# A quarter of V weighted on VectorE and folded on GpSimd, in a decode block with cached keys and values

## The chip, the core and the metric

The kernel runs on one core of a Trainium2 chip. The metric is the device time of one execution in microseconds (us), the median of several runs. A core has five engines that run side by side, each with its own queue of instructions taken in order: TensorE (PE, matrix products), VectorE (DVE), ScalarE (ACT), GpSimd (POOL) and SyncE (SP, which here only issues transfers). Sixteen DMA engines move data between the large memory (HBM) and the core's own memory of 128 partitions. Engines wait for each other by semaphores.

## The reference

Two requests (B = 2), one new token each, width 512, 32 heads of 128, and a cache of 8192 keys and values per head in fp32. The block computes, cut to what matters:

```python
y = layernorm(x)
q = (y @ wq)                       # 32 heads of 128
scores = einsum("bhqd,bhkd->bhqk", q, k_cache) * Dh ** -0.5
p = softmax(scores)
o = einsum("bhqk,bhkd->bhqd", p, v_cache)
h = x + o @ wo                     # wo: 4096 x 512
out = h + gelu(layernorm(layernorm(h)) @ w1 + b1) @ w2 + b2
```

K and V are 268 MB each and are read once. Each value of them is used in one multiplication.

## The kernel before, in words

Two heads and one request make one iteration: 16 pairs of heads times 2 requests are 32 iterations, `i` = 0 to 31. For each, `load` brings a K tile and a V tile of 128 partitions by 128 rows by 128 elements (8.39 MB). Partition `p` of the first 64 belongs to the first head and holds 128 consecutive rows of its cache; the other 64 belong to the second head. Three buffers (`kv`, tag `kv`) go round over wq, K0, V0, K1, V1 and so on, so a tile is loaded when the tile three places before it has been used up: V of iteration i+1 waits for the sums of K of iteration i, and K of iteration i+1 waits for the use of V of iteration i-1. All these loads stand in SyncE's queue in that order, and behind them the weights of the second half (`ws`).

Scores of iteration i are computed in four chunks of 32 rows. `multiply` (line 246) multiplies a chunk of K by q in place on VectorE. `halve` (256) adds the upper 64 elements of each row to the lower 64 on GpSimd, for the rows that `split` gives it (32, 32, 32 and 12), and `sums` (266) reduces what is left on VectorE, one chunk behind. In the last three iterations ScalarE sums some rows too (`by_act`, 260), and GpSimd halves 22, 22, 22 and 8. `row_max` and `all_max` (270 to 280) find the maximum over partitions through TensorE, and `exps` (291) writes the exponentials of the iteration just done into `ptz`, zero-padded to eight columns so that one product serves both heads.

`values(done)` (314) multiplies V of the iteration before by those exponentials: 32 products of 128x8 by 128x512 into four row groups of a PSUM tile `so`. `gather` copies `so` out on ScalarE, `head_sum` (335) adds up the four groups and four column blocks, `head_out` (350) divides by the sum of the exponentials and sets rows in the order in which `turn` and `turned` (358, 367) multiply them by rows of wo. wo comes in nine groups after `PLAN`. Five of them are gathered by an indirect transfer from GpSimd's queue (`load_wo`, 144 and 145) that leaves 32 partitions out, eight blocks of four.

`make_q` (231) spreads q over the partitions with products against `pick`: one call serves two pairs of heads and takes four products, one for each head of a pair and each request. At the end, iteration 31 has its V loaded in four pieces; the softmax, the last products, the two layer norms and the two products with w1 and w2 follow on a chain in which `keep_warm` and `stay_awake` put in products that nobody reads. The order on each engine is that of the program, with `behind` (issue_after) placing one instruction after another. In the loop, `all_max(done)`, `exps(done)` and `values(done)` come ahead of the first `multiply(i, 0)`, and `multiply(i, 0)` is placed behind `all_max`'s reduction.

Of the kernel before, what the change touches and what calls it, by code (L numbers as in the profile page):

```python
# [26 lines left out]
NG = 4  # L27
WARM = 4
MOST = 20
WR = 4  # L30


PLAN = [4, (4, 16, 68, 72, 76, 80, 84, 88),
# [4 lines left out]
FAR = 4096  # L38


# [1 line left out]
def tile_decode_block(ctx: ExitStack, tc: tile.TileContext, x, k, v, wq, wo, w1, b1, w2, b2, out):  # L42
    nc = tc.nc
    B, H, SK, DH = k.shape
    D = x.shape[-1]
    F = w1.shape[1]
    HP = P // QG
    NS = SK // HP
    NC = NS // CH
    DC = D // P  # L50
# [26 lines left out]

    wqt = kv.tile([P, DC, H * DH], F32, name="wqs", tag="kv")
    nc.sync.dma_start(wqt, wq.rearrange("(p r) n -> p r n", r=DC))

    ident = const.tile([P, P], F32, name="ident")
    make_identity(nc, ident)
# [11 lines left out]
    groups, at = [], 0  # L94
    for blocks in PLAN:
        shut = blocks if isinstance(blocks, tuple) else None
        r = WR if shut else blocks
        n = (P - 4 * len(shut or ())) * r
        groups.append((at, n, r, shut))
        at += n  # L100
    assert at == HL * DH
    kept = [[p for p in range(P) if not any(s0 <= p < s0 + 4 for s0 in shut or ())] for _, _, _, shut in groups]
# [4 lines left out]
    part = const.tile([P, 1], F32, name="part")  # L107
# [4 lines left out]
    for _, _, _, blocks in groups:  # L112
        if blocks and blocks not in index:
            acc = work.tile([P, 1], F32, name="ixf")
            nc.vector.tensor_copy(acc, part)
            ends = [p for s0 in blocks for p in (s0, s0 + 4)]
            for p in sorted(set(ends)):
                if ends.count(p) == 1:
                    if p in blocks:
                        edge, step, first = p, FAR, p  # L120
                    else:
                        edge, step = p, first - p - FAR
                    one = work.tile([P, 1], F32, name="ix1")
                    nc.vector.tensor_scalar(one, part, edge - 0.5, float(step), op0=ALU.is_ge, op1=ALU.mult)
                    nc.vector.tensor_add(acc, acc, one)
# [22 lines left out]

    epst = const.tile([P, 1], F32, name="epst")
    nc.vector.memset(epst, EPS)  # L150
    eps2 = const.tile([P, 1], F32, name="eps2")
    nc.vector.memset(eps2, EPS * EPS)
# [6 lines left out]
    QR = 32 * (QG - 1) + B  # L159
# [7 lines left out]
    sel_all = sel.rearrange("p e j -> p (e j)")  # L167
# [5 lines left out]
    nc.vector.memset(sel_row, 0.0)  # L173
    for e in range(QG):
        nc.vector.tensor_copy(sel_row[:, :, 32 * e + B - 1], sel[:, e, :])
    pt2 = const.tile([P, 2, NS // 4, 4 * QG], F32, name="pt")
    nc.gpsimd.memset(pt2, 0.0)
    ptz = [pt2[:, j] for j in range(2)]

    WB = 32 // B  # L180
    otl = const.tile([P, QG, 32], F32, name="otl")
    nc.vector.memset(otl, 0.0)
    place = const.tile([B, 32], F32, name="place")
    nc.vector.memset(place, 0.0)
    nc.vector.tensor_copy(place[:, ::WB], ident[:B, :B])
    sv = const.tile([P, 32], F32, name="sv")
    nc.vector.memset(sv, 0.0)
# [20 lines left out]
    pick = const.tile([P, B, HP], F32, name="pick")  # L208
    nc.vector.tensor_copy(pick, sel_all[:, :B, None].to_broadcast([P, B, HP]))

    QW = H * DH // NG
    q2 = const.tile([P, QW], F32, name="q2")
    for r in range(DC):
        for j in range(QW // 512):
            for n in range(NG):
                nc.tensor.matmul(so2[j][32 * n:32 * n + B], yT[:, r, :],
                                 wqt[:, r, n * QW + j * 512:n * QW + (j + 1) * 512],
                                 start=(r == 0), stop=(r == DC - 1))
    for j in range(QW // 512):
        nc.scalar.activation(q2[:, j * 512:(j + 1) * 512], so2[j], AF.Copy)  # L220

    qps = {}

    def make_q(m):
        n, at = divmod(QG * m * DH, QW)
        t = psq.tile([P, 512], F32, name="qps").rearrange("p (t b d) -> p t b d", t=2, b=B)
        qps[m], qps[m + 1] = t[:, 0], t[:, 1]
        rows = q2[32 * n:32 * n + B, at:at + 2 * QG * DH].rearrange("b (t e d) -> b t e d", t=2, e=QG)
# [9 lines left out]
    ST, MX, MT, GM, GI, LT, RL, SS, OP, TP = {}, {}, {}, {}, {}, {}, {}, {}, {}, {}  # L238
    wl = q2.rearrange("p (e n) -> p e n", e=QG)

    def multiply(i, c):
# [41 lines left out]
    def exps(i):  # L283
        m, b = divmod(i, B)
        nb = work.tile([P, QG], F32, name="nb")
        nc.scalar.activation(nb, GM.pop(i), AF.Copy, scale=SCALE)  # L286
        LT[m] = lt2[:, m % 2]
        s = ST.pop(i).rearrange("p (u j) -> p u j", j=4)
        for e in range(QG):
            ps = slice(e * HP, (e + 1) * HP)  # L290
            nc.scalar.activation(ptz[i % 2][ps, :, 4 * e:4 * e + 4], s[ps], AF.Exp, bias=nb[ps, e:e + 1], scale=SCALE,  # L291
                                 accum_out=LT[m][ps, 32 * e + b:32 * e + b + 1])
# [14 lines left out]
            RL[i] = rl  # L307
            return last

    def values(i, us=range(NS // 4)):  # L310
        so = so2[i % 2]
        for u in us:
            n = u % NG
            m = nc.tensor.matmul(so[32 * n:32 * n + 4 * QG], ptz[i % 2][:, u, :], vt[i][:, 4 * u:4 * u + 4, :],  # L314
                                 start=(u < NG), stop=(u >= NS // 4 - NG))
        return m

    def gather(i):
        SS[i] = work.tile([P, 512], F32, name="ss", bufs=3)
# [50 lines left out]
    def behind(m):  # L370
        return tc.issue_after(m.ins)
# [12 lines left out]
    kt, vt = {}, {}  # L384
# [3 lines left out]
    for i in range(NI):  # L388
        m, b = divmod(i, B)
        done = i - 1  # L390
# [26 lines left out]
        for c in range(NC):  # L417
# [24 lines left out]
            if late and c == 1:  # L442
                spare = psq.tile([P, 512], F32, name="spare", tag="qps")
# [11 lines left out]
        if late:  # L455
            with behind(awake):
                last = values(done, range(MOST))
# [4 lines left out]

    hl = NI - 1
    wt = kv.tile([P, 2, NS * DH // 2], F32, name="ws", tag="kv")
    w1t = wt[:, 0, :DC * F].rearrange("p (c f) -> p c f", c=DC)
    w1v = w1.rearrange("(p c) f -> p c f", c=DC)
    for c in range(0, DC, 2):
# [18 lines left out]
    with behind(after):  # L486
        ended = inverse(hl)
    gather(hl - 1)
    junk = const.tile([P, 2], F32, name="junk")
# [18 lines left out]
    nc.vector.tensor_scalar(basec, base, bmean, None, op0=ALU.subtract)  # L508

    wb = ident.bitcast(BF16)  # L510
    wp = spare[:, :2 * P]

    def keep_warm(n):
        for _ in range(n):
            m = nc.tensor.matmul(wp, wb[:, :P], wb, start=True, stop=True)
        return m


# [51 lines left out]
    hs = pick.rearrange("p b q -> p (b q)")  # L570
# [16 lines left out]
    for c in range(DC):  # L587
# [5 lines left out]
        last = m  # L593
# [57 lines left out]
```

## Time and profile before

| | us |
|---|---|
| median of 3 runs | 1307.65 (1307.62 to 1308.06) |
| span of the profiled execution | 1305.9 |
| its VectorE, GpSimd, TensorE busy | 932.7, 494.2, 446.8 |
| moved by DMA | 561.50 MB, mean 430 GB/s |

The profiled execution has no time of its own beside its span, from the first to the last instruction; the median of the runs is 1.7 us above that span. The page gives the busy time of each engine, the span in 40 slices, the transfer queues, the chain of work that ended last, and the costliest groups of instructions with mean duration and with what ended the idle time before them. "kv<-kv,qps" names the output and the inputs of an instruction; L246 is line 246. Where "x2" follows a row of a timeline, two instructions have been merged into it.

### The profile page before, as it was taken

Reading aid. Unit: us, or ns where it says so; the run is one execution under the profiler, and the core shown is the slowest. Engines: PE = TensorE matmul, PEld = TensorE weight load, DVE = VectorE, ACT = ScalarE, POOL = GpSimd, SP = SyncE. Lnnn points to the kernel's source line nnn. Section 1 sums busy time; section 2 is a strip of 40 time slices with the busy share of each in tenths; the row PEclk is TensorE's granted clock in tenths of the full one; section 3 lists DMA queues with packets and bytes.
Section 4 is the critical chain, followed back from the end, with each engine's and each line's share of the span. In section 5 each row is a group of like instructions: output and inputs, shape, how many; then the busy total and the mean of one; then the engine's idle time right before and its main releaser. Section 6 shows DMA issues by size and latency. Waiting matters only on the chain.

```text
span 1305.9 us, 7466 instructions
## 1 busy us (share of the span) xinstructions
PE 446.8 (34%) x2934; PEld 130.9 (10%) x2934; DVE 932.7 (71%) x551; ACT 98.6 (8%) x431; POOL 494.2 (38%) x151
## 2 busy tenths in 40 slices
PE   3033313333332334413342232333323334123468
PEld 0001001010010101001010010101001011000113
DVE  3666688757688666787766787666787667797891
ACT  0000000000000000000000000000000000004440
POOL 0433344532344432444332454333444433453330
PEclk9566556766566666656766566666666666566689
DMA  9999999999999999999999999999999999999998
GB/s 418 426 440 428 438 422 444 424 440 426 442 426 440 428 438 428 426 444 430 436 426 438 430 434 436 424 442 424 440 426 432 438 432 436 429 428 429 428 434 351
DMA packets 12727, 561.50 MB, mean 430 GB/s; under 512 B 1568, under 2 KB 1584, under 8 KB 2484
## 3 DMA queue, kind: packets, MB, share of 16 engines
q1 hardware_dynamic: 11968, 557.08, 98.8%
q0 software_dynamic: 720, 3.93, 0.7%
q8 instruction: 23, 0.38, 0.1%
q14 instruction: 12, 0.10, 0.0%
q10 hardware_dynamic: 4, 0.00, 0.0%
HBM read 562.32 MB, written 0.00 MB: 431 GB/s over the span
## 4 chain that ended last, share of the span: by engine, by line
DMA 43%; DVE 24%; issue 14%; PE 12%; POOL 5%; ACT 1%; SPq 0%; POOLq 0%; DVEq 0%
DMA kv<-in_A_k_cache_dram 38%; DVE kv L246 14%; PE so L314 10%; DVE s L266 9%; POOL kv L256 5%; DMA kv<-in_A_v_cache_dram 3%; DMA ws<-in_B_w_dram 1%; ACT pt L291 1%; PE rowacc L367 1%; DVE orow L350 1%; PE sm L280 1%; PE sm L273 0%; DVE gm L277 0%; DVE mx L270 0%; ACT nb L286 0%
## 5 line engine op out<-in xcount | busy, mean ns | idle before, releaser
L246 DVE TENSOR_TENSOR kv<-kv,qps 128x4096 f32<-128x4096 f32 x128 | 562.4, 4415 | 313.8 <-DMA kv<-in_A_k_cache_dram 313.6
L256 POOL TENSOR_TENSOR kv<-kv 128x2048 f32<-128x2048 f32 (+3 forms) x128 | 476.8, 3734 | 754.1 <-DVE kv L246 566.3
L266 DVE TENSOR_REDUCE s<-kv 128x32 f32<-128x2048 f32 (+5 forms) x160 | 325.3, 2066 | 10.9 <-POOL kv L256 10.6
L314 PE MATMUL so<-kv,pt 128*8 128x512 f32 x2048 | 280.8, 709 | 42.7 <-ACT pt L291 37.3
L273 PE MATMUL sm<-ident,mx 128*1 128x128 f32 x32 | 10.9, 340 | 446.0 <-DVE mx L270 446.0
L314 PEld LDWEIGHTS so<-kv,pt 128*8 128x8 f32 x2048 | 56.4, 101 | 239.5 <-issue 194.3
L367 PE MATMUL rowacc<-wog,ot 128*2 128x512 f32 x70 | 50.3, 881 | 64.8 <-DVE ot L365 33.4
L286 ACT ACTIVATE nb<-sm 128x2 f32<-128x2 f32 x32 | 5.5, 172 | 851.4 <-PE sm L280 851.4
L231 PE MATMUL qps<-q,pick 2*64 2x256 f32 x64 | 13.8, 577 | 127.6 <-DVE kv L246 127.6
L273 PEld LDWEIGHTS sm<-ident,mx 128*1 128x1 f32 x32 | 2.5, 79 | 472.5 <-issue 278.0
L358 PE MATMUL sm<-ident,orow 2*128 2x2 f32 x35 | 5.2, 244 | 130.1 <-DVE orow L350 130.1
L320 ACT ACTIVATE ss<-so 128x512 f32<-128x512 f32 x31 | 18.5, 598 | 269.6 <-PE so L314 269.6
L260 ACT ACTIVATE kv<-kv 128x128 f32<-128x128 f32 x114 | 33.5, 295 | 24.2 <-DVE kv L246 21.4
L335 PE MATMUL sm<-ss,selr 128*34 128x128 f32 x240 | 28.7, 273 | 0.0
L291 ACT ACTIVATE pt<-s,nb 64x128 f32<-64x128 f32 x64 | 25.5, 399 | 1.4
L335 PEld LDWEIGHTS sm<-ss,selr 128*34 128x34 f32 x240 | 25.1, 112 | 0.0
L260 ACT ACTIVATION_READ_ACCUMULATOR kv<-kv 128x1 f32 x114 | 21.3, 186 | 0.0
L280 PE MATMUL sm<-gm,ones 1*128 1x2 f32 x64 | 16.6, 326 | 11.9 <-DVE gm L277 11.9
L277 DVE TENSOR_REDUCE gm<-sm 1x2 f32<-1x128 f32 x32 | 8.9, 279 | 16.2 <-PE sm L273 16.2
L231 PEld LDWEIGHTS qps<-q,pick 2*64 2x64 f32 x64 | 5.5, 192 | 136.9 <-DVE kv L246 133.2
L358 PEld LDWEIGHTS sm<-ident,orow 2*128 2x128 f32 x35 | 4.4, 207 | 132.6 <-DVE orow L350 79.9
L367 PEld LDWEIGHTS rowacc<-wog,ot 128*2 128x2 f32 x70 | 6.8, 107 | 97.9 <-issue 64.1
(110 smaller groups left out, 169.2 us busy)
## 6 DMA issues: line engine op xcount, KB each, us to landing
kv<-in_A_k_cache_dram SPq DMA_DIRECT2D x4, 4096.0 KB, 32.9
ws<-in_B_w_dram SPq DMA_DIRECT2D x3, 1792.0 KB, 18.5
kv<-in_A_v_cache_dram SPq DMA_DIRECT2D x1, 4096.0 KB, 33.4
wog<-in_A_wo_dram SPq DMA_DIRECT2D x3, 1024.0 KB
kv<-in_A_v_cache_dram SPq DMA_DIRECT2D x1, 2048.0 KB, 37.9
kv<-in_A_v_cache_dram SPq DMA_DIRECT2D x1, 1536.0 KB, 41.2
ws<-in_B_w_dram SPq DMA_DIRECT2D x1, 1024.0 KB, 17.0
wog<-in_A_wo_dram SPq DMA_DIRECT2D x1, 512.0 KB
```

The costliest lines, as they stand in the source:

```text
L231: nc.tensor.matmul(t[e * HP:(e + 1) * HP, :, b], pick[32 * n:32 * n + B, b, :], rows[:, :, e], start=True, stop=True)
L246: return nc.vector.tensor_tensor(kc, kc, qb, op=ALU.mult)
L256: nc.gpsimd.tensor_tensor(t[:, :, :DH // 2], t[:, :, :DH // 2], t[:, :, DH // 2:], op=ALU.add)
L260: nc.scalar.activation(kt[i][:, j, :], kt[i][:, j, :], AF.Copy, accum_out=ST[i][:, j:j + 1])
L266: nc.vector.tensor_reduce(ST[i][:, a:e], kt[i][:, a:e, :d], axis=AX.X, op=ALU.add)
L273: nc.tensor.transpose(MT[i], mx, ident)
L280: GI[i] = nc.tensor.matmul(GM[i], ones[:1, :], gm, start=True, stop=True)
L291: nc.scalar.activation(ptz[i % 2][ps, :, 4 * e:4 * e + 4], s[ps], AF.Exp, bias=nb[ps, e:e + 1], scale=SCALE, accum_out=LT[m][ps, 32 * e + ...
L314: m = nc.tensor.matmul(so[32 * n:32 * n + 4 * QG], ptz[i % 2][:, u, :], vt[i][:, 4 * u:4 * u + 4, :], start=(u < NG), stop=(u >= NS // 4 - ...
L320: return nc.scalar.activation(SS[i], so2[i % 2], AF.Copy)
L335: nc.tensor.matmul(OP[m], sel_row[:, j, B - 1 - c:B - 1 - c + QR], SS[i - 1 + c][:, j * DH:(j + 1) * DH], start=(c == 0 and j == 0), stop= ...
L367: nc.tensor.matmul(rowacc, t[:, r, :], wo_g[g][:, r, :], start=False, stop=(g == len(groups) - 1 and r == n - 1))
```

## The change

1. In iterations 1 to 30, the last 32 of the 128 rows per partition of V are no longer multiplied on TensorE. `weigh` adds the two columns of `ptz` that hold a row's exponential (one of them is zero), multiplies the 32 rows of V by them on VectorE, and GpSimd adds the 32 rows in three steps (16, 8 and 4 rows) down to four. `values_folded` multiplies rows 0 to 95 by 24 products as before, and the four folded rows by one product against `whose`, which is one for the partitions of each head. `multiply(i, 0)` is now placed behind the weighting. The last two values products (iterations 30 and 31) are as before.
2. `make_q`: q of both heads of a pair stand in one row group pair, and one product per request serves both heads (16 products in all where there were 32); wq is read in another order for it.
3. `keep_warm`: products of 512 columns where there were products of 256, half as many.
4. `PLAN`: the 32 partitions left out of each gathered group are given as runs of any length instead of blocks of four.
5. x is loaded on ScalarE's queue after a first square root (which loads ScalarE's table), not as the first instruction of all.
6. `otl`, `sv` and `place` lie in the unused end of the tile `ws` and are set by GpSimd near the end.

The core of the diff:

```diff
-PLAN = [4, (4, 16, 68, 72, 76, 80, 84, 88),
+PLAN = [4, ((10, 18), (51, 3), (73, 3), (84, 8)),
...
-    x2 = work.tile([B, D], F32, name="x2", tag="ss", bufs=3)
-    nc.scalar.dma_start(x2, x.rearrange("b s d -> (b s) d"))
...
+    first = nc.scalar.activation(junk[:, 0:1], eps2, AF.Sqrt)
+    x2 = work.tile([B, D], F32, name="x2", tag="ss", bufs=3)
+    with tc.issue_after(first.ins):
+        nc.scalar.dma_start(x2, x.rearrange("b s d -> (b s) d"))
...
         for b in range(B):
-            for e in range(QG):
-                nc.tensor.matmul(t[e * HP:(e + 1) * HP, :, b], pick[32 * n:32 * n + B, b, :], rows[:, :, e],
-                                 start=True, stop=True)
+            nc.tensor.matmul(t[:, :, b], pick[part, b, :],
+                             q2[part, at:at + 2 * DH].rearrange("r (t d) -> r t d", t=2), start=True, stop=True)
...
+    def weigh(i):
+        w = s_of[i][:, FOLD:].rearrange("p (u j) -> p u j", j=4)
+        pt = ptz[i % 2][:, FOLD // 4:]
+        nc.vector.tensor_tensor(w, pt[:, :, 0:4], pt[:, :, 4:8], op=ALU.add)
+        t = vt[i][:, FOLD:]
+        last = nc.vector.tensor_tensor(t, t, s_of.pop(i)[:, FOLD:, None].to_broadcast([P, NS - FOLD, DH]),
+                                       op=ALU.mult)
+        n = (NS - FOLD) // 2
+        while n >= 4:
+            nc.gpsimd.tensor_tensor(t[:, :n], t[:, :n], t[:, n:2 * n], op=ALU.add)
+            n //= 2
+        return last
+
+    def values_folded(i):
+        so = so2[i % 2]
+        values(i, range(FOLD // 4), range(FOLD // 4 - NG + 1, FOLD // 4))
+        n = FOLD // 4 % NG
+        nc.tensor.matmul(so[32 * n:32 * n + 4 * QG], whose.rearrange("p e j -> p (e j)"), vt[i][:, FOLD:FOLD + 4, :],
+                         start=False, stop=True)
...
             last = all_max(done)
             exps(done)
             if not late:
-                values(done)
+                with behind(last):
+                    last = weigh(done)
+                values_folded(done)
...
-        for _ in range(n):
-            m = nc.tensor.matmul(wp, wb[:, :P], wb, start=True, stop=True)
+        for j in range(0, n, 2):
+            t = min(2, n - j)
+            m = nc.tensor.matmul(wp[:, :t * 2 * P], wb[:, :P], wb[:, None, :].to_broadcast([P, t, 2 * P]),
+                                 start=True, stop=True)
```

More of the change, by code (lines that the diff above doesn't have):

```diff
@@ L79, in tile_decode_block @@
     nc.sync.dma_start(wqt, wq.rearrange("(p r) n -> p r n", r=DC))
+    eps2 = const.tile([P, 1], F32, name="eps2")
+    nc.vector.memset(eps2, EPS * EPS)
+    junk = const.tile([P, 2], F32, name="junk")
+    first = nc.scalar.activation(junk[:, 0:1], eps2, AF.Sqrt)
+    x2 = work.tile([B, D], F32, name="x2", tag="ss", bufs=3)
+    with tc.issue_after(first.ins):
+        nc.scalar.dma_start(x2, x.rearrange("b s d -> (b s) d"))
     ident = const.tile([P, P], F32, name="ident")
@@ L97, in tile_decode_block @@
         r = WR if shut else blocks
-        n = (P - 4 * len(shut or ())) * r
+        n = (P - sum(size for _, size in shut or ())) * r
         groups.append((at, n, r, shut))
@@ L101, in tile_decode_block @@
     assert at == HL * DH
-    kept = [[p for p in range(P) if not any(s0 <= p < s0 + 4 for s0 in shut or ())] for _, _, _, shut in groups]
+    kept = [[p for p in range(P) if not any(s0 <= p < s0 + size for s0, size in shut or ())]
+            for _, _, _, shut in groups]
     group_end = {}
@@ L115, in tile_decode_block @@
             nc.vector.tensor_copy(acc, part)
[L116 to L125, printed above, removed]
+            for s0, size in blocks:
+                for edge, step in ((s0, FAR), (s0 + size, -FAR - size)):
+                    if edge < P:
+                        one = work.tile([P, 1], F32, name="ix1")
+                        nc.vector.tensor_scalar(one, part, edge - 0.5, float(step), op0=ALU.is_ge, op1=ALU.mult)
+                        nc.vector.tensor_add(acc, acc, one)
             index[blocks] = const.tile([P, 1], I32, name=f"ix{len(index)}")
@@ L175, in tile_decode_block @@
         nc.vector.tensor_copy(sel_row[:, :, 32 * e + B - 1], sel[:, e, :])
+    whose = const.tile([P, QG, 4], F32, name="whose")
+    nc.vector.memset(whose, 0.0)
+    for e in range(QG):
+        nc.vector.memset(whose[e * HP:(e + 1) * HP, e], 1.0)
     pt2 = const.tile([P, 2, NS // 4, 4 * QG], F32, name="pt")
@@ L180, in tile_decode_block @@
     WB = 32 // B
[L181 to L187, printed above, removed]
     so2 = [psa.tile([P, 512], F32, name=f"so{j}") for j in range(2)]
@@ L207, in tile_decode_block @@
     nc.vector.tensor_copy(yT, ypt)
-    pick = const.tile([P, B, HP], F32, name="pick")
-    nc.vector.tensor_copy(pick, sel_all[:, :B, None].to_broadcast([P, B, HP]))
+    pick = const.tile([P, B, P], F32, name="pick")
+    nc.vector.memset(pick, 0.0)
+    for n in range(NG):
+        rows, e = slice(32 * n, 32 * n + 32), n % QG
+        nc.vector.tensor_copy(pick[rows, :, e * HP:(e + 1) * HP], sel_all[rows, :B, None].to_broadcast([32, B, HP]))
     QW = H * DH // NG
+    QJ = QW // 512
     q2 = const.tile([P, QW], F32, name="q2")
+    wq_of = wqt.rearrange("p r (f j m e d) -> p r f e j m d", f=NG // QG, j=QJ, e=QG, d=DH)
     for r in range(DC):
-        for j in range(QW // 512):
+        for j in range(QJ):
             for n in range(NG):
-                nc.tensor.matmul(so2[j][32 * n:32 * n + B], yT[:, r, :],
-                                 wqt[:, r, n * QW + j * 512:n * QW + (j + 1) * 512],
+                nc.tensor.matmul(so2[j][32 * n:32 * n + B], yT[:, r, :], wq_of[:, r, n // QG, n % QG, j],
                                  start=(r == 0), stop=(r == DC - 1))
-    for j in range(QW // 512):
+    for j in range(QJ):
         nc.scalar.activation(q2[:, j * 512:(j + 1) * 512], so2[j], AF.Copy)
@@ L224, in make_q @@
     def make_q(m):
-        n, at = divmod(QG * m * DH, QW)
+        f, at = divmod(m * DH, QW)
         t = psq.tile([P, 512], F32, name="qps").rearrange("p (t b d) -> p t b d", t=2, b=B)
         qps[m], qps[m + 1] = t[:, 0], t[:, 1]
-        rows = q2[32 * n:32 * n + B, at:at + 2 * QG * DH].rearrange("b (t e d) -> b t e d", t=2, e=QG)
+        part = slice(64 * f, 64 * f + QR)
         for b in range(B):
-            for e in range(QG):
-                nc.tensor.matmul(t[e * HP:(e + 1) * HP, :, b], pick[32 * n:32 * n + B, b, :], rows[:, :, e],
-                                 start=True, stop=True)
+            nc.tensor.matmul(t[:, :, b], pick[part, b, :],
+                             q2[part, at:at + 2 * DH].rearrange("r (t d) -> r t d", t=2), start=True, stop=True)
     make_q(0)
@@ L287, in exps @@
         LT[m] = lt2[:, m % 2]
-        s = ST.pop(i).rearrange("p (u j) -> p u j", j=4)
+        s_of[i] = ST.pop(i)
+        s = s_of[i].rearrange("p (u j) -> p u j", j=4)
         for e in range(QG):
@@ L308, in inverse, with values @@
             return last
-    def values(i, us=range(NS // 4)):
+    def values(i, us=range(NS // 4), stops=range(NS // 4 - NG, NS // 4)):
         so = so2[i % 2]
@@ L314, in values @@
             m = nc.tensor.matmul(so[32 * n:32 * n + 4 * QG], ptz[i % 2][:, u, :], vt[i][:, 4 * u:4 * u + 4, :],
-                                 start=(u < NG), stop=(u >= NS // 4 - NG))
+                                 start=(u < NG), stop=(u in stops))
         return m
+    def weigh(i):
[16 more added lines that the diff above has]
+                         start=False, stop=True)
     def gather(i):
@@ L464, in tile_decode_block @@
     wt = kv.tile([P, 2, NS * DH // 2], F32, name="ws", tag="kv")
+    misc = wt[:, 0, DC * F:DC * F + P]
+    nc.gpsimd.memset(misc, 0.0)
+    otl = misc[:, 0:32 * QG].rearrange("p (e r) -> p e r", e=QG)
+    sv = misc[:, 32 * QG:32 * QG + 32]
+    place = misc[:B, 32 * QG + 32:]
+    nc.gpsimd.tensor_copy(place[:, ::WB], ident[:B, :B])
     w1t = wt[:, 0, :DC * F].rearrange("p (c f) -> p c f", c=DC)
@@ L510, in tile_decode_block @@
     wb = ident.bitcast(BF16)
-    wp = spare[:, :2 * P]
+    wp = spare
     def keep_warm(n):
-        for _ in range(n):
-            m = nc.tensor.matmul(wp, wb[:, :P], wb, start=True, stop=True)
+        for j in range(0, n, 2):
+            t = min(2, n - j)
+            m = nc.tensor.matmul(wp[:, :t * 2 * P], wb[:, :P], wb[:, None, :].to_broadcast([P, t, 2 * P]),
+                                 start=True, stop=True)
         return m
```

7 lines of the change are left out of this document (3 added, 4 removed), and 8 rows, old and new, of the table PLAN.

## The prediction

> **What bounds the kernel now.** The page comes first: shares, queues, span.
>
> ```profile
> span 1305.9 us, 7466 instructions
> PE 446.8 (34%) x2934; PEld 130.9 (10%) x2934; DVE 932.7 (71%) x551; ACT 98.6 (8%) x431; POOL 494.2 (38%) x151
> DMA packets 12727, 561.50 MB, mean 430 GB/s; under 512 B 1568, under 2 KB 1584, under 8 KB 2484
> q1 hardware_dynamic: 11968, 557.08, 98.8%
> q8 instruction: 23, 0.38, 0.1%
> ```
>
> The DMA engines work for 98.8% of the span on one queue: 561.5 MB at 430 GB/s is 1306 us, the whole time. An 8.39 MB tile of K or V takes 19.5 us at that rate. VectorE at 71% looks loose, but that is an average; the question is how long one turn of its loop takes. The timeline of two turns (start, duration, what; the bracket is the idle time before it) shows that.
>
> ```profile
> 129.81 2.29 DVE L266 TENSOR_REDUCE s<-kv 128x32 f32<-128x2048 f32 x1 [0.30 <-POOL kv L256]
> 149.75 0.29 DVE L270 TENSOR_REDUCE mx<-s 128x1 f32<-128x128 f32 x1
> 152.70 9.69 PE L314 MATMUL so<-kv,pt 128*8 128x512 f32 x64 [1.28 <-ACT pt L291]
> 161.80 8.75 DVE L246 TENSOR_TENSOR kv<-kv,qps 128x4096 f32<-128x4096 f32 x2 [11.02 <-DMA kv<-in_A_k_cache_dram]
> 166.44 4.53 POOL L256 TENSOR_TENSOR kv<-kv 128x2048 f32<-128x2048 f32 x1 [20.62 <-DVE kv L246]
> 171.00 2.29 DVE L266 TENSOR_REDUCE s<-kv 128x32 f32<-128x2048 f32 x1 [0.45 <-POOL kv L256]
> 189.95 0.29 DVE L270 TENSOR_REDUCE mx<-s 128x1 f32<-128x128 f32 x1
> ```
>
> The reader is to see the gap: the row maximum of iteration 2 starts at 149.75, the first multiply of iteration 3 at 161.80, and the 11 us between are a wait for K. So the loop has about 11 us to spare. The SyncE queue shows the same from the other side: it issues a load as soon as a buffer is released, and the next load of V goes out with the row maximum.
>
> ```profile
> 70.65 0.33 SPq L75 DMA_DIRECT2D kv<-in_A_v_cache_dram  x1
> 149.74 0.33 SPq L75 DMA_DIRECT2D kv<-in_A_v_cache_dram  x1
> 162.46 0.33 SPq L75 DMA_DIRECT2D kv<-in_A_k_cache_dram  x1
> ```
>
> V of iteration 2 goes out at 149.74, though the transfer engines reach it only when K of iteration 2 has landed, at 161.80: 12 us in hand. K of iteration 3 goes out at 162.46, with a whole V tile (19.5 us) queued before it. The last iterations and the end:
>
> ```profile
> 1184.65 8.75 DVE L246 TENSOR_TENSOR kv<-kv,qps 128x4096 f32<-128x4096 f32 x2 [8.86 <-DMA kv<-in_A_k_cache_dram]
> 1193.32 1.61 DVE L266 TENSOR_REDUCE s<-kv 128x22 f32<-128x1408 f32 x1
> 1209.53 0.29 DVE L270 TENSOR_REDUCE mx<-s 128x1 f32<-128x128 f32 x1
> 1215.34 8.75 DVE L246 TENSOR_TENSOR kv<-kv,qps 128x4096 f32<-128x4096 f32 x2 [4.68 <-DMA kv<-in_A_k_cache_dram]
> 1224.09 1.59 DVE L266 TENSOR_REDUCE s<-kv 128x22 f32<-128x1408 f32 x1
> 1241.53 0.28 DVE L270 TENSOR_REDUCE mx<-s 128x1 f32<-128x128 f32 x1
> 1267.59 0.29 DVE L270 TENSOR_REDUCE mx<-s 128x1 f32<-128x128 f32 x1
> ...
> 1274.96 3.62 PE L314 MATMUL so<-kv,pt 128*8 128x512 f32 x32 [0.63 <-DMA kv<-in_A_v_cache_dram]
> 1283.56 2.37 PE L314 MATMUL so<-kv,pt 128*8 128x512 f32 x16 [0.16 <-DMA kv<-in_A_v_cache_dram]
> 1293.75 1.71 PE L590 MATMUL so<-ws,ones 128*32 128x448 f32 x16 [0.48 <-DMA ws<-in_B_w_dram]
> 1300.55 1.08 PE L620 MATMUL po<-ws,pt 128*32 128x128 f32 x32 [0.68 <-DMA ws<-in_B_w_dram]
> 1301.79 1.07 PE L620 MATMUL po<-ws,pt 128*32 128x128 f32 x24 [0.16 <-DMA ws<-in_B_w_dram]
> ```
>
> From one first multiply that waited for K (161.80) to another (1184.65) are 26 turns: 39.34 us each, the pace of DMA. At the end TensorE waits for data only 0.63 + 0.16 + 0.48 + 0.68 + 0.16 = 2.1 us in all: a softmax that comes later than that moves the end.
>
> **The fold of V, part by part.** In every iteration from 1 to 30 VectorE gets two instructions between the maximum over partitions and the first multiply, and GpSimd three adds ahead of its first halving. Both engines take them in order, so they join the loop. The rows that price them:
>
> ```profile
> L246 DVE TENSOR_TENSOR kv<-kv,qps 128x4096 f32<-128x4096 f32 x128 | 562.4, 4415 | 313.8 <-DMA kv<-in_A_k_cache_dram 313.6
> L256 POOL TENSOR_TENSOR kv<-kv 128x2048 f32<-128x2048 f32 x87 | 392.0, 4518 | 624.1 <-DVE kv L246 468.2 <-issue 97.8 <-PE sm L335 58.2
> L256 POOL TENSOR_TENSOR kv<-kv 128x768 f32<-128x768 f32 x29 | 52.5, 1809 | 71.6 <-DVE kv L246 45.7 <-DVE ot L365 25.9
> L256 POOL TENSOR_TENSOR kv<-kv 128x1408 f32<-128x1408 f32 x9 | 28.6, 3177 | 49.2 <-DVE kv L246 47.1 <-DVE rlr L306 1.1 <-DVE rl L306 1.0
> L256 POOL TENSOR_TENSOR kv<-kv 128x512 f32<-128x512 f32 x3 | 3.8, 1272 | 9.2 <-DVE kv L246 5.4 <-DVE ot L365 3.9
> L125 DVE TENSOR_TENSOR ixf<-ixf,ix 128x1 f32<-128x1 f32 x34 | 5.2, 153 | 0.4
> ```
>
> The chain of waits gives the handover between the engines:
>
> ```profile
> 42.64 4.43 DVE kv L246
> 47.15 4.53 POOL kv L256
> 51.70 2.29 DVE s L266
> ```
>
> VectorE to GpSimd 0.08 us (47.07 to 47.15), back 0.02. Call W the end of the weighting. One turn from W to the next W is then:
> - three adds of 2048, 1024 and 512 elements: 4.52, 2.35 (on the line through 2048 and 768) and 1.27, each behind the one before; with 0.08 ahead of each, 8.38;
> - the first halving, which stands behind them on GpSimd: 4.53, and 0.02 to VectorE. The first two multiplies (8.75) run meanwhile;
> - from the first sum to the maximum 18.95 (171.00 to 189.95); with a head's output 19.94 (129.81 to 149.75), more where pieces are many. Half the turns have one: 19.50;
> - maximum to exponentials done 2.95 (149.75 to 152.70);
> - the add of two columns, as a small VectorE instruction 0.2 with its handover, and the weighting of 4096 elements, 4.42: 4.62.
>
> The sum is 40.00, against 39.34 for DMA. The loop no longer fits: from the first iteration on it sets the pace itself, because halving waits for the adds even when K is there. The Trainium skill (GPSIMD Engine Reference, section 3.1) gives 4497 ns for an add of 2048 fp32 elements on GpSimd; no row here has an add of contiguous elements. By it the first add would be 0.02 us shorter and the sum of all turns some 0.6 us, an estimate. The Trainium skill (VectorE: DVE Perf Modes, section on the TRN2 errata) has (N+151)/0.96 ns for an fp32 tensor_tensor, 4.42 us for 4096 elements, where no row has both operands in SBUF; that agrees with the 4415 ns of line 246.
>
> Run through: the first maximum at 70.65 gives W = 70.65 + 2.95 + 4.62 = 78.2, and 28 turns later, in iteration 29, W = 1198.2. There the halving is the short one: 8.38 + 3.18 + 0.02, then 16.21 (1193.32 to 1209.53), maximum at 1226.0 instead of 1209.53: 16.5 late. Iteration 30: W at 1233.6, first sum at 1245.2, 17.44 more (1224.09 to 1241.53), 1262.6 instead of 1241.53: 21.1 late. Iteration 31 has no weighting and no slack, so the last maximum (1267.59) is also 21.1 late. Of this the end absorbs its 2.1 us of waiting.
>
> Does DMA keep up with 40.0? V goes out at the maximum and K of the iteration after it lands two tiles (39 us) later; it is needed 47.6 us after that maximum. DMA idles but isn't what is waited for. The fold's one product stands on TensorE behind 24 others; with about 1 us for it (line 314's instructions, two to a product, at 9.69 us for 64 in the row above, and a cold start), K of the next iteration goes out 7.57 + 8.38 + 1 = 17 us after the maximum instead of 12.7 (162.46), still well within the 19.5 us of the V tile queued before it. Behind it on TensorE stand the head sums, on ScalarE the copy of the product, on SyncE the load of K: all wanted only later in the turn. Without that cover the product would cost its own length, 30 times.
>
> **The rest.** Seven products per iteration less (of 32), half of the q products and about half of the keep-warm instructions: TensorE fetches about 940 of 5868 instructions less, a sixth of the 0.38 MB of queue q8, 0.14 us of DMA. Wider unread products stand on the late chain of the end; 40 became 21 and spare about 0.5 us of it.
>
> ```profile
> L515 PE MATMUL spare<-ident 128*128 128x256 bf16 x40 | 5.7, 273 | 0.0
> PE so L216 <- DMA wqs<-in_A_wq_dram: 15.2, 1, 15.2
> ```
>
> The rows of wo left out number 32 per gather as before: same bytes, distributed otherwise. That can only even out transfer engines that DMA time no longer depends on: 0. Twelve more index steps of two small instructions (0.3 us each) in front, the table load ahead of x, and one q layout more: TensorE waits 15.2 us for wq there, which hides them; without that cover they cost 4 to 5 us. Six more pieces of head output: a turn's pieces together cost 0.99 us (19.94 less 18.95), so six spread over 15 such turns stay under 0.2 us a turn; 0 taken. The setting of small tiles on GpSimd at the end falls into its idle time.
>
> Sum: +21.1 - 2.1 - 0.5 = +18.5 us on a span of 1305.9. The median of the runs, 1307.65, is 1.7 above the span; with the same 1.7 the forecast is 1326 us, 1.4% slower.
>
> **Rivals.** *The loop still fits (not slower).* If the three adds with their handovers take 7.7 us or less instead of 8.38, a turn is at most 39.34 and DMA sets the pace as before. For it: contiguous operands instead of strided ones, and a margin of only 0.66. Against it: the line through three lengths of one operation. Then only iteration 30 is serial: W at 1209.53 + 7.57 = 1217.1, first sum 10.9 later at 1228.0 instead of 1224.09, 3.9 late, less 2.6: about 1309.
> *A longer handover.* GpSimd waits for itself between the adds; the nearest row has 0.28 there instead of 0.08.
>
> ```profile
> POOL wog L145 <- POOL wog L144: 1.4, 5, 0.3
> ```
>
> Twice 0.2 more per turn, 30 turns: +12, 1338.
> *The change does only what it saves* (0.14 of fetches, finer balance; the softmax at the end hidden): 1307. Against it stand the 2.1 us of the end.
>
> **How the numbers follow.** Forecast 0.53 (own range 1316 to 1334: 0.3 us per turn either way), longer handover 0.2, loop fits 0.23, savings alone 0.04. Range 1308 to 1338. The measurement of this kernel tells 0.2%, 2.6 us, from no change: slower is forecast and longer handover with a little of the fit's upper side, 0.75; same 0.22; faster 0.03.
>
> **What would show it.** First multiplies that wait for the weighting and first sums that wait 4 us for GpSimd; turns of 40.0 us; idle time of DMA in the second half; a last maximum near 1289. Wrong, if first multiplies still wait for K throughout, or if the adds sum to under 7.7.

## The result, and the profile after

| | before | after |
|---|---|---|
| median (lowest to highest), 5 runs each, us | 1307.66 (1307.62 to 1308.06) | 1327.91 (1327.22 to 1328.68) |
| span of the profiled execution | 1305.9 | 1326.7 |

The ratio of after to before is 1.0156, with a 95% interval of 1.0145 to 1.0167: 1.6% slower; the slowest run of before and the fastest of after lie 19.2 us apart. The profiled execution of the changed kernel itself took 1328.5 us, 0.6 above the median, so between the two profiles the span grows by 20.8 us where the medians differ by 20.2. The page of the changed kernel, with the lines that answer to those of before:

```profile
span 1326.7 us, 6749 instructions
PE 478.1 (36%) x2463; PEld 130.7 (10%) x2463; DVE 1073.5 (81%) x643; ACT 98.7 (7%) x432; POOL 738.3 (56%) x243
DMA packets 12725, 561.45 MB, mean 423 GB/s; under 512 B 1568, under 2 KB 1584, under 8 KB 2484
q1 hardware_dynamic: 11968, 557.08, 97.8%
q8 instruction: 19, 0.31, 0.1%
...
DVE 53%; POOL 28%; PE 7%; DMA 6%; issue 4%; ACT 3%; POOLq 0%; SPq 0%; DVEq 0%
```

The last line is the chain that ended last, as shares of the span. Before the change its line read:

```profile
DMA 43%; DVE 24%; issue 14%; PE 12%; POOL 5%; ACT 1%; SPq 0%; POOLq 0%; DVEq 0%
```

DMA falls from 43% of the chain to 6%, and VectorE and GpSimd together rise from 29% to 81%. Yet no engine is full: VectorE is busy for 81% of the span, GpSimd for 56%. The groups of instructions of the changed kernel (busy time, mean ns; then the idle time before them and what ended it) show what lies between:

```profile
L246 DVE TENSOR_TENSOR kv<-kv,qps 128x4096 f32<-128x4096 f32 x128 | 562.2, 4413 | 30.7 <-DMA kv<-in_A_k_cache_dram 30.3
L324 DVE TENSOR_TENSOR kv<-kv,s 128x4096 f32<-128x4096 f32 x30 | 132.7, 4424 | 1.0
L328 POOL TENSOR_TENSOR kv<-kv 128x2048 f32<-128x2048 f32 x30 | 136.8, 4559 | 317.4 <-DVE kv L324 317.4
L328 POOL TENSOR_TENSOR kv<-kv 128x1024 f32<-128x1024 f32 x30 | 70.8, 2360 | 2.4
L328 POOL TENSOR_TENSOR kv<-kv 128x512 f32<-128x512 f32 x30 | 38.1, 1271 | 2.3
L266 DVE TENSOR_REDUCE s<-kv 128x32 f32<-128x2048 f32 x87 | 198.5, 2282 | 108.7 <-POOL kv L256 108.4
```

The multiplies by q (L246) waited 313.6 us for K before; now they wait 30.3, all of it before 280 us. In their place the halved sums (L266) wait 108.4 us for GpSimd's halving. Their row before:

```profile
L266 DVE TENSOR_REDUCE s<-kv 128x32 f32<-128x2048 f32 x87 | 198.5, 2282 | 10.8 <-POOL kv L256 10.6
```

One turn in the timeline of the changed kernel (rows of VectorE and GpSimd, some between them left out; start, duration, the idle time before in brackets):

```profile
592.03 0.29 DVE L270 TENSOR_REDUCE mx<-s 128x1 f32<-128x128 f32 x1
595.28 4.42 DVE L324 TENSOR_TENSOR kv<-kv,s 128x4096 f32<-128x4096 f32 x1
599.63 8.74 DVE L246 TENSOR_TENSOR kv<-kv,qps 128x4096 f32<-128x4096 f32 x2
599.79 8.35 POOL L328 TENSOR_TENSOR kv<-kv 128x2048 f32<-128x2048 f32 x3 [11.69 <-DVE kv L324]
608.10 8.97 POOL L256 TENSOR_TENSOR kv<-kv 128x2048 f32<-128x2048 f32 x2
612.63 2.29 DVE L266 TENSOR_REDUCE s<-kv 128x32 f32<-128x2048 f32 x1 [4.19 <-POOL kv L256]
632.73 0.29 DVE L270 TENSOR_REDUCE mx<-s 128x1 f32<-128x128 f32 x1
635.58 4.42 DVE L324 TENSOR_TENSOR kv<-kv,s 128x4096 f32<-128x4096 f32 x1
```

The reader sees the new loop. The weighting ends at 599.70; GpSimd adds three times and only then halves the chunk that VectorE has had ready since about 604; VectorE is done with two multiplies at 608.37 and, after one small instruction of 0.15 us, stands still for 4.19 us until 612.63. This turn, from weighting to weighting, takes 40.30 us; the one before it, without a head's output, began at 555.74 and took 39.54. Both are longer than the 39.34 us of a turn that DMA paced before the change. The first weighting, and the last iterations:

```profile
72.62 1.28 ACT L292 ACT_TABLE_LOAD   x1
75.17 4.42 DVE L324 TENSOR_TENSOR kv<-kv,s 128x4096 f32<-128x4096 f32 x1
...
1196.39 4.42 DVE L324 TENSOR_TENSOR kv<-kv,s 128x4096 f32<-128x4096 f32 x1
1228.61 0.29 DVE L270 TENSOR_REDUCE mx<-s 128x1 f32<-128x128 f32 x1
1265.35 0.28 DVE L270 TENSOR_REDUCE mx<-s 128x1 f32<-128x128 f32 x1
1267.34 0.28 DVE L277 TENSOR_REDUCE gm<-sm 1x2 f32<-1x128 f32 x1 [1.70 <-PE sm L273]
1292.48 0.29 DVE L270 TENSOR_REDUCE mx<-s 128x1 f32<-128x128 f32 x1
1320.34 3.26 PE L650 MATMUL po<-ws,pt 128*32 128x128 f32 x112 [1.08 <-DVE pt L647]
```

The last maximum comes 24.9 us later than before (1267.59), and the last products, at 1320.34, no longer wait for weights.

### The profile page after: what moved, and what is told of

It reads as the page before. It is cut to its first block, busy times and chain, and to the rows that moved or that the text cites. A ratio compares the mean times of both kernels' runs of the same rounds, so it can differ in the third digit from the quotient of the medians.

```text
span 1326.7 us, 6749 instructions
## 1 busy us (share of the span) xinstructions
PE 478.1 (36%) x2463; PEld 130.7 (10%) x2463; DVE 1073.5 (81%) x643; ACT 98.7 (7%) x432; POOL 738.3 (56%) x243
## 4 chain that ended last, share of the span: by engine, by line
DVE 53%; POOL 28%; PE 7%; DMA 6%; issue 4%; ACT 3%; POOLq 0%; SPq 0%; DVEq 0%
DVE kv L246 22%; DVE s L266 19%; POOL kv L328 18%; POOL kv L256 10%; DVE kv L324 10%; DMA kv<-in_A_k_cache_dram 6%; PE rowacc L388 3%; ACT pt L292 2%; PE sm L280 1%; DVE orow L371 1%; PE sm L273 1%; PE so L315 1%; DVE gm L277 1%; DVE mx L270 1%; DVE s L322 0%
## 5 line engine op out<-in xcount | busy, mean ns | idle before, releaser
L246 DVE TENSOR_TENSOR kv<-kv,qps 128x4096 f32<-128x4096 f32 x128 | 562.2, 4413 | 30.7 <-DMA kv<-in_A_k_cache_dram 30.3
L328 POOL TENSOR_TENSOR kv<-kv 128x2048 f32<-128x2048 f32 (+2 forms) x90 | 245.7, 2730 | 322.1 <-DVE kv L324 317.4
L266 DVE TENSOR_REDUCE s<-kv 128x32 f32<-128x2048 f32 (+5 forms) x160 | 325.4, 2067 | 114.5 <-POOL kv L256 114.2
L315 PE MATMUL so<-kv,pt 128*8 128x512 f32 x1568 | 237.8, 765 | 39.9 <-ACT pt L292 37.3
L324 DVE TENSOR_TENSOR kv<-kv,s 128x4096 f32<-128x4096 f32 x30 | 132.7, 4424 | 1.0
L336 PE MATMUL so<-kv,whose 128*8 128x512 f32 x60 | 56.2, 1041 | 155.9 <-POOL kv L328 155.9
L388 PE MATMUL rowacc<-wog,ot 128*2 128x512 f32 x70 | 54.8, 952 | 65.2 <-DVE ot L386 65.2
L315 PEld LDWEIGHTS so<-kv,pt 128*8 128x8 f32 x1568 | 45.3, 106 | 203.4 <-issue 163.6
L322 DVE TENSOR_TENSOR s<-pt 128x32 f32<-128x32 f32 x30 | 5.8, 192 | 56.8 <-ACT pt L292 56.8
L230 PE MATMUL qps<-q,pick 34*128 34x256 f32 x32 | 14.4, 600 | 94.5 <-DVE kv L246 94.5
L356 PE MATMUL sm<-ss,selr 128*34 128x128 f32 x240 | 44.4, 347 | 10.3 <-ACT ss L341 10.3
L356 PEld LDWEIGHTS sm<-ss,selr 128*34 128x34 f32 x240 | 31.4, 143 | 39.6 <-ACT ss L341 36.9
```

Source lines behind the costliest of these rows:

```text
L246: return nc.vector.tensor_tensor(kc, kc, qb, op=ALU.mult)
L266: nc.vector.tensor_reduce(ST[i][:, a:e], kt[i][:, a:e, :d], axis=AX.X, op=ALU.add)
L324: last = nc.vector.tensor_tensor(t, t, s_of.pop(i)[:, FOLD:, None].to_broadcast([P, NS - FOLD, DH]), op=ALU.mult)
L328: nc.gpsimd.tensor_tensor(t[:, :n], t[:, :n], t[:, n:2 * n], op=ALU.add)
L336: nc.tensor.matmul(so[32 * n:32 * n + 4 * QG], whose.rearrange("p e j -> p (e j)"), vt[i][:, FOLD:FOLD + 4, :], start=False, stop=True)
L356: nc.tensor.matmul(OP[m], sel_row[:, j, B - 1 - c:B - 1 - c + QR], SS[i - 1 + c][:, j * DH:(j + 1) * DH], start=(c == 0 and j == 0), stop= ...
```

## The experiments

The theory: the fold alone costs the 20 us, and in it not the work that VectorE gets but the stall, because GpSimd's three adds stand in its queue ahead of the first halving. The rivals: VectorE's weighting by itself is too much, GpSimd's total work is, or the other parts of the change add to the loss. The times below are medians; those beside them of the kernel before, on the same chip, are 1307.7 us. Every kernel here computes the whole block.

**1. The other parts, without the fold.**

```diff
             if not late:
-                with behind(last):
-                    last = weigh(done)
-                values_folded(done)
+                values(done)
```

> All parts of the change but the fold: values are summed on TensorE as before, 16 products an iteration. Theory (the fold alone costs the 20 us): the transfers pace the loop again at 39.3 us a turn, the time is 1306.5 to 1308 us, and VectorE's halved sums wait for GpSimd about 11 us in all, not 108. Rival (the other parts lose some of it, through the rows of wo, the later x, or the products of q): 1310 us or more. Rival (the other parts save what the prediction gave them, 0.5 us for the wide keep-warm and 0.1 us for the instructions): 1307.0 us; by the rows of keep-warm after the change, which are as long as before, 1307.5 us is likelier.

Measured: 1308.89 us (1308.48 to 1309.72, 11 runs), ratio 1.001 with an interval of 1.0001 to 1.0019. The waits of this kernel (who waits, for whom; us in all, times, the longest):

```profile
DVE kv L246 <- DMA kv<-in_A_k_cache_dram: 306.3, 31, 20.6
```

VectorE waits for K again, 31 times, and its halved sums wait 10.6 us for GpSimd, as expected. So the 20 us go with the fold. But the other parts save nothing: they cost 1.2 us, above the 1306.5 to 1308 us of the theory and below the 1310 us of the rival, so neither range held. Experiments 7 to 9 look for that.

**2. The fold alone**, put into the kernel before: the code of `whose`, `weigh` and `values_folded`, and their call in the loop.

> The kernel before with the fold alone, everything else as before. Theory: 1328 us (1327 to 1329.5), a turn of 40.0 us, and the wait of VectorE's halved sums for GpSimd at 4.2 us an iteration. Rival (the rest contributes to the loss): under 1326 us.

Measured: 1327.18 us (1326.68 to 1327.56), ratio 1.015 (1.0134 to 1.0165).

```profile
DVE s L272 <- POOL kv L262: 112.0, 31, 4.3
```

The halved sums (here line 272) wait 112.0 us for GpSimd over all their forms, up to 4.3 us at a time, as in the changed kernel. The fold gives 19.5 of the 20.2 us.

**3. The same work, with the halved sums two chunks behind their multiply.**

```diff
+        lag = 2 if 0 < i < NI - 1 else 1
...
-                if c > 0:
-                    sums(i, c - 1, True)
+                if c >= lag:
+                    sums(i, c - lag, True)
                 sums(i, c, False)
...
-        sums(i, NC - 1, True)
+        for c in range(NC - lag, NC):
+            sums(i, c, True)
```

> The changed kernel with the order of VectorE's work altered in the loop: the halved sums come two chunks behind their multiply, so that VectorE does its third multiply (4.41 us) in the time in which it stood waiting 4.2 us for the first halving. Nothing is added or left out. Theory (the stall behind GpSimd's adds, not the weighting itself, takes the turn past the transfers): a turn of work falls from 40.0 to about 36 us, the transfers pace it again at 39.3 us, VectorE waits for K from DMA each iteration as before the change, and the time is 1307 to 1310 us. Rival (the weighting, 4.42 us on VectorE ahead of the next maximum, is enough by itself): 1320 to 1328 us. Rival (GpSimd's 25 us of adds an iteration are the chain, whatever VectorE's order): 1325 to 1330 us.

Measured: 1307.62 us (1307.36 to 1309.18, 11 runs), ratio 1.0002 (0.9993 to 1.0011). The whole loss is gone, though VectorE and GpSimd do just what they do in the changed kernel. (Six of the eleven runs take 1307.36 to 1307.62 us and five 1308.50 to 1309.18; against 20 us that spread does not matter, but it does for experiments 7 to 11.) A turn of this kernel, first VectorE's timeline with GpSimd's (some rows left out), then the groups:

```profile
626.39 4.42 DVE L324 TENSOR_TENSOR kv<-kv,s 128x4096 f32<-128x4096 f32 x1
630.89 8.33 POOL L328 TENSOR_TENSOR kv<-kv 128x2048 f32<-128x2048 f32 x3 [13.55 <-DVE kv L324]
633.41 13.08 DVE L246 TENSOR_TENSOR kv<-kv,qps 128x4096 f32<-128x4096 f32 x3 [2.59 <-DMA kv<-in_A_k_cache_dram]
639.18 13.49 POOL L256 TENSOR_TENSOR kv<-kv 128x2048 f32<-128x2048 f32 x3
646.41 2.28 DVE L266 TENSOR_REDUCE s<-kv 128x32 f32<-128x2048 f32 x1
661.02 0.29 DVE L270 TENSOR_REDUCE mx<-s 128x1 f32<-128x128 f32 x1
```

```profile
L246 DVE TENSOR_TENSOR kv<-kv,qps 128x4096 f32<-128x4096 f32 x128 | 560.9, 4413 | 124.0 <-DMA kv<-in_A_k_cache_dram 123.8
L266 DVE TENSOR_REDUCE s<-kv 128x32 f32<-128x2048 f32 x87 | 198.3, 2279 | 0.6 <-POOL kv L256 0.3
L324 DVE TENSOR_TENSOR kv<-kv,s 128x4096 f32<-128x4096 f32 x30 | 132.7, 4425 | 1.0
```

VectorE does its third multiply (three in 13.08 us) while GpSimd adds and halves; the first sum at 646.41 finds its chunk ready. The wait for GpSimd falls from 108.4 to 0.3 us, and the wait for K comes back: 123.8 us in all, some 3.5 us a turn after the first, which is 21.0. So a turn of work takes 39.3 - 3.5 = 35.8 us, about the 36 expected, and DMA sets the pace again. This rules out both rivals: VectorE is as busy as after the change, and so is GpSimd (737.6 us).

**4. The quarter weighted on VectorE but not folded on GpSimd**; TensorE sums the eight weighted blocks with `whose`.

```diff
-        n = (NS - FOLD) // 2
-        while n >= 4:
-            nc.gpsimd.tensor_tensor(t[:, :n], t[:, :n], t[:, n:2 * n], op=ALU.add)
-            n //= 2
...
+        for u in range(FOLD // 4, NS // 4):
+            n = u % NG
+            nc.tensor.matmul(so[32 * n:32 * n + 4 * QG], whose.rearrange("p e j -> p (e j)"),
+                             vt[i][:, 4 * u:4 * u + 4, :], start=False, stop=(u >= NS // 4 - NG))
```

> The changed kernel with the quarter of V weighted on VectorE as in the change, but not folded on GpSimd: TensorE sums the eight weighted blocks by eight products with the same table of heads. Theory (GpSimd's three adds, 8.4 us, ahead of its first halving are the cause, by VectorE's wait of 4.2 us): the turn of work is 40.0 - 4.2 = 35.8 us, below the 39.3 us of the transfers, and the time is 1307 to 1310 us. Rival (VectorE's 4.42 us of weighting is the cause): 1320 to 1328 us.

Measured: 1308.78 us (1308.38 to 1309.30, 10 runs). The groups of this kernel:

```profile
L246 DVE TENSOR_TENSOR kv<-kv,qps 128x4096 f32<-128x4096 f32 x128 | 562.4, 4415 | 112.4 <-DMA kv<-in_A_k_cache_dram 112.2
L266 DVE TENSOR_REDUCE s<-kv 128x32 f32<-128x2048 f32 x87 | 198.5, 2282 | 10.9 <-POOL kv L256 10.6
```

With the weighting in place and GpSimd's adds gone, K is waited for again, and the halved sums wait 10.6 us as before the change. The weighting eats slack, 313.6 us down to 112.2, but not time.

**5 and 6. An eighth and a half of V in place of a quarter**: the changed kernel with one size altered, `FOLD = 112` and `FOLD = 64`.

> The changed kernel with an eighth of V folded in place of a quarter: the weighting is 2048 elements wide (about 2.3 us) and GpSimd's adds are 1024 and 512 (2.36 and 1.27 us). Theory: GpSimd is done 3.8 us after the weighting ends, before VectorE's first multiply is (4.4 us), so the halved sums don't wait; the turn of work is about 33 to 34 us, the transfers pace it at 39.3 us, and the time is 1307 to 1308.5 us. Rival (the loss is in proportion to what is folded): about half of the 20 us, 1317 us.

Measured: 1308.51 us (1307.41 to 1308.68, 10 runs), with 174.6 us of waiting for K and 9.1 us for GpSimd. Not half of the loss but none of it, beyond what the other parts cost.

> The changed kernel with half of V folded: the weighting is 8192 elements wide (8.69 us, 4.27 more) and GpSimd has one more add, of 4096 elements (8.9 us by twice the 2048 one). Theory (weighting, then GpSimd's adds, then its first halving stand in one chain of the turn): a turn of 40.0 + 4.27 + 8.9 = 53.2 us, and a time of about 1328 + 30 x 13.2 = 1724 us. Rival (the adds lie beside VectorE's own work, only the weighting counts): a turn of 44.3 us and 1328 + 30 x 4.3 = 1457 us.

Measured: 1720.64 us, a single run. A turn of this kernel (some rows left out):

```profile
606.72 8.69 DVE L324 TENSOR_TENSOR kv<-kv,s 128x8192 f32<-128x8192 f32 x1
615.49 17.21 POOL L328 TENSOR_TENSOR kv<-kv 128x4096 f32<-128x4096 f32 x4 [15.90 <-DVE kv L324]
637.18 2.29 DVE L266 TENSOR_REDUCE s<-kv 128x32 f32<-128x2048 f32 x1 [13.11 <-POOL kv L256]
659.42 8.69 DVE L324 TENSOR_TENSOR kv<-kv,s 128x8192 f32<-128x8192 f32 x1
```

This turn, without a head's output, is 52.70 us, where one without it took 39.54 in the changed kernel; over the 16 turns from the weighting at 340.29 to the one at 1190.88 the mean is 53.16 (53.2 expected). The weighting is longer by 4.27 us, and the stall grew from 4.25 (before the sum at 573.08 of the changed kernel) to 13.11, by the 8.9 us of the one new add. All of the added length lies on the chain. An eighth is free, a quarter costs 1.6%, a half 32%: the cost begins where a turn of work passes the pace of DMA, and from there on every microsecond on the chain counts 30 times.

**7 to 9. Where the other parts lose 1.2 us.** Three kernels without the fold: with the old rows of wo, the kernel before with only the new rows, and with x loaded first.

```diff
-PLAN = [4, ((10, 18), (51, 3), (73, 3), (84, 8)),
+PLAN = [4, (4, 16, 68, 72, 76, 80, 84, 88),
```

> All parts of the change but the fold, and with the rows of wo left out as in the kernel before (blocks of four partitions). Without the fold the other parts gave 1308.9 us, 1.2 us above the kernel before; in that run the last weights land about 1 us later and TensorE's products are as long as before, so the transfers take the 1.2 us. Theory (the new choice of rows loads the 16 DMA engines less evenly, although it moves the same bytes): 1307.3 to 1307.9 us. Rival (the later load of x, or what VectorE and SP do at the start): 1308.5 to 1309.2 us.

Measured: 1307.66 us (1307.54 to 1309.07, 11 runs).

> The kernel before with the new choice of rows of wo alone. Theory (the rows cost 1.2 us on a kernel paced by its transfers): 1308.5 to 1309.2 us. Rival (they cost nothing, or balance the engines better): 1306.8 to 1307.9 us.

Measured: 1308.58 us (1308.42 to 1308.71, 11 runs; the 33 runs of the kernel before go from 1307.42 to 1308.24).

> All parts of the change but the fold, and with x loaded first, as in the kernel before. If the rows of wo carry the 1.2 us: 1308.5 to 1309.2 us. If the later load of x does (it puts small packets between the first large ones of wq and K): 1307.3 to 1307.9 us.

Measured: 1308.51 us (1308.41 to 1309.57, 11 runs).

Taking the new rows away takes the loss away, putting them in alone brings 0.9 us, and the load of x changes little. So in these kernels without the fold the choice of rows carries about 1 us, with the same number of bytes. The ratios' intervals (0.9991 to 1.0009, 0.9997 to 1.0015, 0.9998 to 1.0016) do not part these kernels from the one before; the ranges of the runs of experiment 9 and of the kernel before do not overlap, and on that the reading rests. It is not a fixed price, though: experiment 3 has the new rows too and DMA paces it, and six of its eleven runs lie within 0.1 us of the range of the kernel before, the other five about 1 us higher. How the rows load the sixteen engines the trace does not tell apart, so why they cost it stays open.

**10 and 11. A version that could beat both.** Experiment 3 without the weighting in iteration 30, where TensorE alone sums the values, so that no weighting stands ahead of the last maxima; and the same with the old rows.

```diff
-                with behind(last):
-                    last = weigh(done)
-                values_folded(done)
+                if i < NI - 2:
+                    with behind(last):
+                        last = weigh(done)
+                    values_folded(done)
+                else:
+                    values(done)
```

> The kernel with the halved sums two chunks behind, and with the values of the last iteration but one summed on TensorE alone, so that no weighting stands ahead of the last maxima. Theory: the loop is paced by the transfers and the end is that of the kernel before: 1306.5 to 1308 us, at most 0.05% below the kernel before. Rival (the last iterations keep some of the loss by the late K buffers): 1308 to 1312 us.

Measured: 1308.53 us (1307.26 to 1308.69, 11 runs: five up to 1307.72, six from 1308.53).

> The changed kernel with the halved sums two chunks behind, the values of the last iteration but one summed on TensorE alone, and the rows of wo left out as in the kernel before. If the rows carry the 1.2 us, this kernel loses them: 1307.0 to 1307.7 us. If not: 1307.3 to 1308.7 us, as with the new rows. Below the kernel before by more than 0.2% in neither case, since the transfers pace both.

Measured: 1308.11 us (1307.86 to 1308.42, 11 runs).

Neither beats the kernel before. The median of the first is half a microsecond above its expectation, but with runs that lie 0.8 us apart in two groups, a single run more in the lower one would have moved it to 1307.7. The second contradicts experiment 8 in part: with the fold the old rows do not reach the 1307.0 to 1307.7 us expected, and its median lies above that of experiment 3, which has the new rows. The cost of a choice of rows depends on the rest of the kernel; on what, these runs do not show.

## Why the prediction was right, point by point

The forecast was 1326 us, the time is 1327.91; the likeliest case is what happened, and the working can be held against the trace term by term.

- **The price of the stall: right.** From the end of the weighting to the first halved sum the sum had 8.38 + 4.55 = 12.93 us; the trace has 599.70 to 612.63, 12.93. The line through three lengths of strided halvings, used for adds of contiguous rows, had 4.52, 2.35 and 1.27; the means are 4.56, 2.36 and 1.27. The figure of the Trainium skill (GPSIMD Engine Reference, section 3.1) for the first add, 4497 ns, would have made it shorter than the halving; the changed kernel has 4559 ns for it, so the halvings were the better price. The Trainium skill (VectorE: DVE Perf Modes, section on the TRN2 errata) has (N+151)/0.96 ns for an fp32 tensor_tensor add; an estimate by it for the weighting, a multiply of 4096 elements, is 4.42 us. The trace agrees with 4424 ns.
- **The rest of the turn: right to 0.1%.** First sum to maximum 18.95 without a head's output (573.08 to 592.03), as taken; with it 20.10 in the turn shown, where 19.94 was taken. Over the 28 turns from W = 79.59 to W = 1200.81 a turn is 40.04 us, where 40.00 was forecast.
- **"The loop still fits": fell.** The adds with their handovers would have had to take 7.7 us; they take 8.4 (599.70 to the halving at 608.10). Its condition was well placed, though: experiments 3 to 5 take the turn below 39.34, and each gets the time back.
- **A longer handover on GpSimd: fell.** The three adds merge to 8.35 us for 8.19 us of mean durations, 0.08 between one and the next.
- **The first weighting: missed by 1.4 us.** W was put at 78.2 and is 79.59. Maximum to exponentials was taken from a later turn; in the first one ScalarE loads its table (1.28 us in the row above). It was there before as well, hidden by the wait for K.
- **The last iterations: right up to iteration 30, then 1.1 us short.** Weighting to maximum takes 27.80 us in iteration 29 (27.79 forecast) and 29.07 in iteration 30 (29.0). Iteration 31 was to add nothing, but VectorE's reduction there waits 1.70 us for TensorE, and from maximum to maximum it takes 27.13 us, 26.06 before. Ahead of the product that it waits for, TensorE has eight products with rows of wo (line 388, line 367 before), which take 6.11 us where they took 5.00; that is the 1.1 us. The granted clock over them is 0.50 from 1260.9 to 1265.0 and 0.74 from there to 1267.1; before it was 0.50 from 1237.2 to 1239.0, 0.73 to 1241.0 and 1.00 to their end. Together with the first weighting and the turns the last maximum is 24.9 us late, where 21.1 was forecast.
- **What the end absorbs: mis-sized.** It was put at 2.1 us of waiting for data and 0.5 for wider unread products. The span grew by 20.8, so 4.1 were absorbed. The waits for data are gone, and products between them run closer together: the last 112 took 4.72 us from first to last before (1298.14 to 1302.86) and take 3.26, 1.46 less, where the two waits named there came to 0.84. Two more pieces that the sum did not have: sixteen of the last products with V took 2.37 us and take 1.90, and from the last maximum to the reduction over partitions 1.19 us became 0.74. Some 0.4 of the 4.1 is spread in smaller pieces. The wider unread products gave nothing: the largest group takes 1.47 us for six, where twelve took 1.48.

```profile
1317.79 1.47 PE L544 MATMUL spare<-ident 128*128 128x512 bf16 x6
```

- **"The rest" of the change at nothing: right for the changed kernel, wrong as a rule.** Between the fold alone (1327.18) and the whole change (1327.91) lie 0.7 us. In the kernels without the fold, which DMA paces, the new rows of wo cost about 1 us (experiments 7 to 9), where 0, or a gain, was argued. That the start's added steps are hidden holds: TensorE still waits 11.1 us for wq, 15.2 before.
- **DMA idles but is not waited for: half shown.** V goes out with the maximum, as said, and K's waits have all but gone. But the row of the windows view for the middle of the run has the DMA share (next to last) at 1.00 in both kernels; only the rate falls, from 433 to 427 GB/s. Before, then after:

```profile
600.00:900.00 300.00, 86.97 (x563) 25.01 (x563) 225.30 (x104) 12.26 (x42) 125.54 (x35) 0.64 1.00 433
```

```profile
600.00:900.00 300.00, 103.93 (x505) 28.10 (x497) 249.30 (x115) 12.85 (x43) 184.57 (x58) 0.61 1.00 427
```

- **K's buffer 17 us after the maximum: 18.** The product of the folded rows was put at 1 us; it is two instructions of 1.04 us, 1.88 us together at 608.20. It lies beside other work, as said.

The two misses at the front and at iteration 31 (3.8 us late together with the turns) and the one at the end (1.5 us more absorbed) went opposite ways, so the forecast is closer than its terms.

## What to carry to other kernels

Work given to an engine with spare time is free only up to the slack of one turn of the loop, and what counts against that slack is the chain through all the engines, with each queue's order, and not the busy share of any of them. Before a change is given up, ask whether the stall that it makes can be filled by moving work that is already there: here one multiply moved ahead of the sums gave back the whole 20 us with not an instruction less. Where DMA sets the pace all along, as here, taking work off TensorE gives no time back: none of the eleven kernels of the experiments is faster than the kernel before, and the best medians (experiments 3 and 8) are within 0.1 us of its own.

## What the runs showed of the hardware that was not expected

A product on TensorE right behind others and the same product after a wait differ, and the granted clock differs with them. The product of the folded rows against `whose` takes 593 ns an instruction in experiment 5, where it follows 28 others at once, and 1041 ns in the changed kernel, after a wait for GpSimd (155.9 us over 30 of them). In experiment 6, after waits of up to 22.7 us, it is 1041 ns too: the longer wait adds nothing. The granted clock around one of these products is 1.00 in experiment 5 (632.50 to 633.50 us), and 0.50 in the changed kernel (608.20 to 609.30) and in experiment 6 (632.60 to 634.50): at half the clock the instruction takes 1.76 times as long. Here are the changed kernel and experiment 5:

```profile
L336 PE MATMUL so<-kv,whose 128*8 128x512 f32 x60 | 56.2, 1041 | 155.9 <-POOL kv L328 155.9
```

```profile
L336 PE MATMUL so<-kv,whose 128*8 128x512 f32 x60 | 30.7, 593 | 0.7
```

The other is the rows of wo: gathers of the same size, with other partitions left out, moved the end of a kernel without the fold, paced by DMA, by about 1 us (experiments 8 and 9); with the fold the runs do not bear it out (experiments 3 and 11).
